# One tile of probabilities for the 64-row third chunks of a pair's two heads

## The chip, the cores and the metric

The kernel runs on 1 core of one Trainium2 chip. The metric is device time in microseconds (us) of one execution; 1089.18 is the median of three runs of the kernel before.

## The reference

Causal softmax attention over 4 x 8 heads of 576 positions with 64 columns each, mixed with a memory read-out by a gate per head, and behind it two feed-forward layers over 2304 tokens of 512 columns, with 2048 hidden units each:

```python
scores = scale * np.matmul(q, k.transpose(0, 1, 3, 2))      # then causal mask, minus the row's maximum
a = np.exp(scores)
a /= a.sum(-1, keepdims=True) + 1e-09
local = np.matmul(a, v)
q_p = phi(q)                                                # x > 0: x + 1, else exp(x)
mem_out = (q_p @ M_prev) / ((q_p * z_prev).sum(-1) + 1e-06)
attn = g * mem_out + (1 - g) * local                        # g = sigmoid(beta), one per head
h = x @ w_in;  x = elu(h) @ w_out                           # first layer
h = x @ w2_in; x = np.maximum(0.01 * h, h) @ w2_out         # second layer
```

## The kernel before

**Tiles.** The batch has four entries; in each, heads are taken in four pairs, 16 pairs in all. The 576 query rows of a head are cut into five chunks of 128, 128, 64, 128 and 128 rows (`CH`); the third has only 64. A pair's work falls into four *items*: for the first head chunks 0 and 1 (first group) and chunks 2, 3 and 4 (second group), and the same for the second head. So a pair's items are, in order, head 0 group 0, head 0 group 1, head 1 group 0, head 1 group 1.

**One item.** `score` makes for each chunk a matmul of queries and keys on PE (TensorE), a masked minimum on DVE (VectorE, line 431), which also writes the scores to the tile `pt`, and an exponential on ACT (ScalarE, line 436), which also sums each row. `norm` turns the sums into factors (rs, lines 445 and 446) and scales `pt` by them and by one minus the head's gate (`omg`) on POOL (GpSimd, line 451). `tr` transposes 128x128 pieces of `pt` on PE (line 457). In the second group `t1(0)`, `t1(1)` and `t1c` each transpose one block of keys of chunks 2, 3 and 4 into one bank, and the bank is split into a rounded part and a remainder by ACT and DVE (`ah`, `al`, `ac`, lines 247 to 250). `pv` multiplies them with the values (*value product*, line 524) and adds the memory read-out; its result goes to DRAM (`xq`). The first batch entry works in float32 without the split.

**Third chunk.** Its tile `pt2` holds 128 rows, of which 64 are used and the others stay zero. Each head has its own exponential, scaling and transposes for it.

**The first layer beside attention.** When a batch entry's attention is done, its tokens (two *parts* of 288 for each entry, parts 0 to 7) go through the first 7 blocks of hidden units of the first layer while the next entry's attention runs. A hidden unit is 12 matmuls on line 620, an output unit 21 on line 648. `u_load` brings the tokens in, `u_x` adds and rounds them (`xh`, `xl`, line 610). What is left over, and the rest of both layers with 512 tokens at a time, comes after attention. Weights are brought in as pairs of words and decoded by ACT, DVE and POOL (lines 112 to 137).

**Order.** The program lays units down one after another: `weave` mixes the scores of item n, the transposes of item n - 1 and the value product of item n - 2 by their place in their lists, and units of the first layer are put between them as the added costs of attention units give credit. From that a scheduler sets the order on each engine when the kernel is built, but an instruction marked to stay in program order (the first chunk's add and rounding in `u_x` and `split_x`) keeps its place. Each engine then works strictly in its order. DMAs are issued by SP (SyncE).

**Buffers.** `pt2` has two buffers, which alternate by item; `ah`, `al` and `ac` have two each, one for each item of the second group.

## Time and profile before

| | |
|---|---|
| median of 3 runs | 1089.18 us (1088.93 to 1090.98) |
| the profiled execution's own time | 1091.76 us |
| its span, first to last instruction | 1090.0 us |
| PE busy | 1052.7 us (97%) |
| DVE busy | 592.8 us (54%) |
| POOL busy | 527.5 us (48%) |
| ACT busy | 484.4 us (44%) |
| attention's last value product | at 394 us |
| mean granted clock of PE | 0.992 |

The clock of PE has two levels, 1.2 and 2.4 GHz; 1.00 is the higher one. PE counts as busy from a matmul's start to its modelled end, and ends overlap the next start, so what a matmul costs PE is read from the distance of starts. An idle time is followed by what ended it: "4.26 <-ACT xh L610" means that the engine had nothing to do for 4.26 us until ACT wrote xh on line 610.

### The profile page before, as it was taken

How to read it: one execution, taken by the hardware profiler on the slowest of the kernel's cores; microseconds unless marked ns; L12 is line 12 of the kernel's file. 1: busy time of each engine (PE TensorE's matmuls, PEld its weight loads, DVE VectorE, ACT ScalarE, POOL GpSimd, SP SyncE). 2: the span in 40 equal slices, each digit the busy share in tenths (PEclk: the TensorE clock that was granted, in tenths of full speed). 3: DMA queues.
4: the chain of work that ended last, by engine and by line, in shares of the span. 5: the costliest groups of instructions: out<-in, count | busy, mean ns of one | idle time of the engine just before them, and what ended most of it. 6: DMA issues, size and time to landing. Idle time of an engine off the chain costs nothing.

```text
span 1090.0 us, 17393 instructions
## 1 busy us (share of the span) xinstructions
PE 1052.7 (97%) x5904; PEld 912.6 (84%) x5904; DVE 592.8 (54%) x1398; ACT 484.4 (44%) x1169; POOL 527.5 (48%) x674
## 2 busy tenths in 40 slices
PE   6998999999999989999999999999999999999997
PEld 3786799989989989988777889888888888888896
DVE  6889987788878646566663214754321221232232
ACT  5899887777878534544342223432211211111110
POOL 7665776677667526555342234855422322222221
PEclk9999999999999999999999999999999999999999
DMA  7654543465445257666563304431200100000010
GB/s 181 186 150 113 161 141 98 123 167 147 119 122 145 88 168 228 219 207 203 170 208 97 112 5 117 142 112 37 78 1 1 58 20 1 6 34 1 1 39 20
DMA packets 151576, 115.05 MB, mean 106 GB/s; under 512 B 81728, under 2 KB 144192, under 8 KB 151488
## 3 DMA queue, kind: packets, MB, share of 16 engines
q1 hardware_dynamic: 151488, 113.95, 35.5%
q8 instruction: 47, 0.77, 0.3%
q14 instruction: 41, 0.34, 0.1%
HBM read 78.52 MB, written 31.85 MB: 101 GB/s over the span
## 4 chain that ended last, share of the span: by engine, by line
PE 74%; DVE 9%; DMA 8%; POOL 3%; issue 2%; ACT 2%; SPq 2%; DVEq 0%; POOLq 0%; ACTq 0%
PE pm L620 16%; PE sc L886 14%; PE tp L620 13%; PE sc L648 6%; PE pm L648 4%; PE po L886 4%; PE po L524 3%; PE tp L457 3%; DMA x1s<-st 2%; PE pm L524 2%; DMA y<-xq 2%; PE po L648 2%; PE sc L426 1%; PE sc L428 1%; DVE pt L431 1%
## 5 line engine op out<-in xcount | busy, mean ns | idle before, releaser
L627 POOL TENSOR_TENSOR gl<-e,gh 128x512 fp32r<-128x512 f32 (+2 forms) x181 | 198.2, 1097 | 383.8 <-DVE gh L243 287.0
L620 PE MATMUL tp<-xw,w 128*128 128x512 f32 (+1 forms) x504 | 145.1, 369 | 0.0
L620 PE MATMUL pm<-xw,w 128*128 128x512 f32 (+1 forms) x496 | 143.9, 371 | 0.4 <-DVE e L634 0.4
L886 PE MATMUL sc<-w,gh 128*128 128x512 f32 x448 | 137.6, 393 | 0.0
L451 POOL TENSOR_SCALAR pt<-pt,rs,omg 128x128 f32<-128x128 f32 (+4 forms) x160 | 101.9, 645 | 25.2 <-DVE rs L446 20.8
L648 PE MATMUL sc<-gh,w 128*128 128x512 f32 (+2 forms) x438 | 107.2, 343 | 3.3 <-DVE st L867 2.2
L620 PEld LDWEIGHTS pm<-xw,w 128*128 128x128 f32 x496 | 90.7, 188 | 18.2 <-DVE e L634 0.9
L620 PEld LDWEIGHTS tp<-xw,w 128*128 128x128 f32 x504 | 91.6, 188 | 16.8
L436 ACT ACTIVATE pt<-pt,mx 128x128 f32<-128x128 f32 (+4 forms) x160 | 93.1, 583 | 17.9 <-DVE mx L431 17.1
L886 PEld LDWEIGHTS sc<-w,gh 128*128 128x128 f32 x448 | 83.1, 188 | 17.8
L620 PE MATMUL tp<-xv,w 128*128 128x512 f32 (+1 forms) x252 | 92.7, 368 | 0.0
L620 PE MATMUL pm<-xv,w 128*128 128x512 f32 (+1 forms) x248 | 91.7, 370 | 0.0
L639 ACT ACTIVATE e<-pm 128x512 f32<-128x512 f32 (+1 forms) x40 | 22.2, 555 | 150.0 <-PE pm L620 148.6
L243 DVE CAST gh<-e 128x512 fp32r<-128x512 f32 (+2 forms) x146 | 76.7, 527 | 18.0 <-PE po L648 4.9
L648 PEld LDWEIGHTS sc<-gh,w 128*128 128x128 f32 x438 | 74.7, 188 | 13.9 <-issue 3.4
L886 PE MATMUL sc<-w,gl 128*128 128x512 f32 x224 | 85.4, 393 | 0.0
L457 PE MATMUL tp<-ident,pt 128*128 128x128 f32 x480 | 81.9, 281 | 3.4 <-ACT ah L247 2.1
L137 POOL TENSOR_TENSOR w<-wm,w 128x512 fp32r<-128x512 f32 x50 | 65.4, 1330 | 40.8 <-ACT w L241 40.2
L640 DVE TENSOR_TENSOR e<-tp,e 128x512 f32<-128x512 f32 (+1 forms) x40 | 25.5, 637 | 106.2 <-ACT e L639 106.0
L640 DVE TENSOR_TENSOR e<-pm,e 128x512 f32<-128x512 f32 (+1 forms) x40 | 25.5, 636 | 106.0 <-ACT e L639 106.0
L620 PE MATMUL pm<-xh,w 128*128 128x288 f32 x368 | 79.9, 305 | 0.3 <-DVE e L634 0.3
L431 DVE CUSTOM_DVE_ANT_0 pt<-sc,mask 128x128 f32<-128x128 f32 (+4 forms) x160 | 69.3, 446 | 8.6 <-PE sc L429 3.6
(155 smaller groups left out, 2400.3 us busy)
## 6 DMA issues: line engine op xcount, KB each, us to landing
wraw<-in_moe_w_in_dram SPq DMA_DIRECT2D x32, 512.0 KB, 4.1
wraw<-in_moe_w_out_dram SPq DMA_DIRECT2D x32, 512.0 KB, 5.2
xh<-xh SPq DMA_DIRECT2D x8, 576.0 KB, 3.1
xl<-xl SPq DMA_DIRECT2D x8, 576.0 KB, 3.8
ys<-st SPq DMA_DIRECT2D x32, 144.0 KB, 2.9
x1s<-st SPq DMA_DIRECT2D x36, 128.0 KB, 1.9
x<-x1s SPq DMA_DIRECT2D x9, 512.0 KB, 4.1
out_dram<-st SPq DMA_DIRECT2D x36, 128.0 KB, 1.7
```

The source lines that it names most:

```text
L137: nc.gpsimd.tensor_tensor(out=w[:, 1, a], in0=t[:, a], in1=_f(w)[:, 0, a], op=ALU.subtract)
L243: (nc.vector if eng == "V" else nc.gpsimd).tensor_copy(dst, src)
L431: nc.vector.tensor_tensor_reduce(out=pt[0:m, k0:k0 + n], in0=sc[0:m, 0:n], in1=mk, op0=ALU.add, op1=ALU.min, scale=-0.125, scalar=mx[0:m, ...
L436: nc.scalar.activation(out=pt[0:m, 0:nk], in_=pt[0:m, 0:nk], func=AF.Exp, scale=-1.0, bias=mx[0:m, last:last + 1], accum_out=self.pd["ss"] ...
L451: nc.gpsimd.tensor_scalar(out=pt, in0=pt, scalar1=rs[0:m, i:i + 1], scalar2=omg[0:m, h:h + 1], op0=ALU.mult, op1=ALU.mult,)
L457: nc.tensor.transpose(dst, self.p[c][:, k0:k0 + kn], ident)
L524: nc.tensor.matmul(po[:, a:b], w, x, start=i == 0, stop=i == len(mms) - 1)
L620: nc.tensor.matmul(ph, wi[:, wj, kc, :], xx[:, kc, :], start=n_mm == 0, stop=n_mm == 11)
L627: nc.gpsimd.tensor_tensor(out=gl, in0=g, in1=_f(gh), op=ALU.subtract)
L640: nc.vector.tensor_tensor(out=t, in0=ph, in1=t, op=ALU.max)
L648: nc.tensor.matmul(py, wo[:, wj, ec * P:(ec + 1) * P], gg, start=opens and f == first and n_mm == 0, stop=closes and f == last and n_mm == 2,)
L886: nc.tensor.matmul(pos[tb], gg[:, tb * P:(tb + 1) * P], wo[:, wj, :], start=f == 0 and n_mm == 0, stop=f == NF - 1 and n_mm == 2,)
```

## The change

The third chunks of both heads of a pair share `pt2`: head 0 in rows 0 to 63, head 1 in rows 64 to 127. Both score matmuls and minimums (`score2`) are done in the item of head 0 and group 1, and one exponential over 128 rows follows. One scaling over 128 rows takes a new table `omp`, which holds the gate factor of head 0 in the upper rows and that of head 1 in the lower. In `t1` and `t1c` the item of head 0 transposes the shared tile with chunks 3 and 4: the 64 columns of head 0 go to the front of the bank and those of head 1 to its end. The item of head 1 transposes only chunks 3 and 4. `ah`, `al` and `ac` belong to the pair: 640 columns, one buffer, written as 384 columns by head 0's item and as 256 by head 1's. The value products read 320 columns each, as before.

```diff
+    omp = const.tile([P, H // 2], F32, name="omp")
+    for j in range(2):
+        nc.vector.tensor_copy(omp[64 * j:64 * j + 64], omg.rearrange("p (h j) -> p j h", j=2)[64 * j:64 * j + 64, j])
...
+        def score2(self, j):
+            pr = self.pr
+            c0, m = CH[2]
+            nk = c0 + m
+            r = slice(64 * j, 64 * j + 64)
...
+            if j == 0:
+                self.p[2] = pads[self.n // 4 % 2]["pt2"]
+                self.mx2 = at.tile([P, 2], F32, tag="mx", bufs=4, name="mx")
+            pt, mx = self.p[2], self.mx2
+            sc = bank("sc")[:, 0:nk]
+            qc = qs[:, c0 - 64 * j:c0 - 64 * j + P]
...
+            o = 448 - c0 + 64 * j
+            nc.vector.tensor_tensor_reduce(
+                out=pt[r, 0:nk], in0=sc[r], in1=mask[r, o:o + nk], op0=ALU.add, op1=ALU.min,
+                scale=-0.125, scalar=1e38, accum_out=mx[r, 0:1],
+            )
+            if j == 1:
+                nc.scalar.activation(
+                    out=pt[:, 0:nk], in_=pt[:, 0:nk], func=AF.Exp, scale=-1.0, bias=mx[:, 0:1],
+                    accum_out=self.pd["ss"][:, 2:3],
+                )
...
+                og = omp[:, self.pr.hp:self.pr.hp + 1] if c == 2 else omg[:, h:h + 1]
                 nc.gpsimd.tensor_scalar(
-                    out=pt, in0=pt, scalar1=rs[0:m, i:i + 1], scalar2=omg[0:m, h:h + 1],
-                    op0=ALU.mult, op1=ALU.mult,
+                    out=pt, in0=pt, scalar1=rs[:, i:i + 1], scalar2=og, op0=ALU.mult, op1=ALU.mult,
                 )
...
+        def tr1(self, k0):
+            ps = bank("tp")
+            if self.j == 0:
+                self.tr(ps[:, 0:384].rearrange("p (b n) -> p b n", n=64)[:, 0:6:5], 2, k0, 128)
+            o = 64 if self.j == 0 else 0
+            for c in (3, 4):
+                self.tr(ps[:, o:o + P], c, k0, 128)
+                o += P
+            a = 384 * self.j
+            return ps[:, 0:o + 64 * (1 - self.j)], slice(a, a + o + 64 * (1 - self.j))
...
+            if kc == 0 and self.j == 0:
+                pr.ah = at.tile([P, 2, 640], F32R, tag="ah", name="ah")
+                pr.al = at.tile([P, 2, 640], F32R, tag="al", name="al")
+            split(pr.ah[:, kc, at_], pr.al[:, kc, at_], src, pr.full_v)
...
-            a = [(cost[c], lambda c=c: self.score(c)) for c in cc] + [(0, self.norm)]
+            a = [(cost[2], lambda j=j: self.score2(j)) for j in range(2)] if 2 in self.cc else []
+            a += [(cost[c], lambda c=c: self.score(c)) for c in cc if c != 2] + [(0, self.norm)]
```

The order on the engines changes with it. Three places follow.

POOL, the first pair, from the row factors of its second and third item on. Before:

```order
L445 TENSOR_SCALAR rs<-ss_152 128x3
L445 TENSOR_SCALAR rs<-ss_160 128x2
L243 COPY vv<-vn 128x640
L451 TENSOR_SCALAR pt_171<-pt_171,rs,omg 64x320
L451 TENSOR_SCALAR pt_309<-pt_309,rs,omg 128x448
L451 TENSOR_SCALAR pt_315<-pt_315,rs,omg 128x576
L396 TENSOR_TENSOR ph_e<-ph_f,den 128x640
```

The same place now:

```order
L474 TENSOR_SCALAR rs<-ss_155 128x3
L474 TENSOR_SCALAR rs<-ss_163 128x2
L399 TENSOR_TENSOR ph_e<-ph_f,den 128x640
L480 TENSOR_SCALAR pt_174<-pt_174,rs,omp 128x320
L480 TENSOR_SCALAR pt_315<-pt_315,rs,omg 128x448
L480 TENSOR_SCALAR pt_321<-pt_321,rs,omg 128x576
L246 COPY vv<-vn 128x640
```

The copy of the second pair's values (vv from vn, which a DMA brings) has moved behind the scaling of the second item.

PE, where the first hidden unit of part 2 begins (xh0_3628, on line 620, is its rounded tokens; dh0, dh1 and dh2 are the split tiles of three items in turn, here of the first, second and third item of the pair). Before:

```order
L457 MATMUL tp_3664<-ident_66,pt1_3482 128x128
L524 MATMUL po_3537<-qph_3467,ms1_183 128x256
L524 MATMUL po_3537<-qpl_3468,ms1_183 128x256
L524 MATMUL po_3537<-dh0_140,vv_3282 128x256
L524 MATMUL po_3537<-dh0_140,vv_3282 128x128
L524 MATMUL po_3537<-dl0_142,vv_3282 128x256
L524 MATMUL po_3537<-dl0_142,vv_3282 128x128
L428 MATMUL sc_3765<-kk0_3567,qs0_3655 128x256
L429 MATMUL sc_3765<-kl0_0_164,qs0_3655 128x256
L620 MATMUL pm_3670<-xh0_3628,w0_204 128x288 x2
```

The same place now, with the tokens xh0_3559 on line 658:

```order
L485 MATMUL tp_3819<-ident_66,pt1_3674 128x128
L561 MATMUL po_3681<-qph_3389,ms1_186 128x256
L561 MATMUL po_3681<-qpl_3390,ms1_186 128x256
L561 MATMUL po_3681<-dh2_159,vv_3206 128x256
L561 MATMUL po_3681<-dh2_159,vv_3206 128x128
L561 MATMUL po_3681<-dl2_161,vv_3206 128x256
L561 MATMUL po_3681<-dl2_161,vv_3206 128x128
L457 MATMUL sc_3855<-kk1_3484,qs1_3572 128x256
L458 MATMUL sc_3855<-kl1_0_169,qs1_3572 128x256
L658 MATMUL pm_3599<-xh0_3559,w0_207 128x288 x2
```

The hidden unit now comes after the value product of the pair's third item (dh2) and no longer after that of the first (dh0): the value products of two items have moved ahead of it.

ACT, right after attention: the rounding of part 6's tokens (xh_6577, three chunks together and then the first chunk, which keeps its place in the program), the decoding of a weight (wm, w) and copies of outputs of part 5 (st). Before:

```order
L610 CAST xh_6577<-x 128x288 x3
L126 ACTIVATE wm<-wraw 128x1024
L241 COPY st<-sc 128x288 x2
L610 CAST xh_6577<-x 128x288
L241 CAST w_6658<-wm 128x1024
```

The same place now:

```order
L648 CAST xh_6432<-x 128x288 x3
L129 ACTIVATE wm<-wraw 128x1024
L244 COPY st<-sc 128x288 x2
L244 CAST w_6513<-wm 128x1024
L244 COPY st<-sc 128x288 x2
L648 CAST xh_6432<-x 128x288
```

The first chunk's cast now stands behind all four output copies of part 5 and a weight's cast. Before, two of the four copies stood ahead of this whole place.

## Rows read from the trace of the kernel before

**Rows 1.** The page's totals: engine, busy us (share of the span), instructions.
```profile
PE 1052.7 (97%) x5904; PEld 912.6 (84%) x5904; DVE 592.8 (54%) x1398; ACT 484.4 (44%) x1169; POOL 527.5 (48%) x674
```
**Rows 2.** Busy us by window: length, PE, PEld, DVE, ACT, POOL, PEclk, DMA, GB/s.
```profile
100.00:110.00 10.00, 7.80 (x41) 5.70 (x40) 9.10 (x24) 9.19 (x26) 7.21 (x13) 0.83 0.63 157
...
120.00:130.00 10.00, 8.17 (x52) 7.13 (x52) 9.52 (x26) 8.07 (x23) 8.08 (x13) 0.83 0.57 159
```
**Rows 3.** Groups by line and shape: count | busy us, mean ns | idle before, releasers.
```profile
L457 PE MATMUL tp<-ident,pt 128*128 128x128 f32 x480 | 81.9, 281 | 3.4 <-ACT ah L247 2.1 <-DVE dl L250 0.4 <-DVE al L250 0.3
...
L436 ACT ACTIVATE pt<-pt,mx 128x448 f32<-128x448 f32 x32 | 21.4, 669 | 1.7 <-DVE mx L431 1.4
...
L436 ACT ACTIVATION_READ_ACCUMULATOR pt<-pt,mx 128x1 f32 x128 | 24.6, 193 | 0.0
...
L451 POOL TENSOR_SCALAR pt<-pt,rs,omg 64x320 f32<-64x320 f32 x32 | 19.5, 610 | 16.6 <-DVE rs L446 13.0 <-DVE den L394 1.2 <-DVE den L393 1.1
...
L436 ACT ACTIVATE pt<-pt,mx 64x320 f32<-64x320 f32 x32 | 17.9, 561 | 5.3 <-DVE mx L431 5.3
...
L436 ACT ACTIVATE pt<-pt,mx 128x256 f32<-128x256 f32 x32 | 16.3, 508 | 2.6 <-DVE mx L431 2.5
```
**Rows 4.** Timeline of PE, attention of the first entry: start us, duration us, instruction.
```profile
57.48 0.49 PE L457 MATMUL tp<-ident,pt 128*128 128x128 f32 x3
57.80 0.70 PE L524 MATMUL pm<-ah,vv 128*128 128x320 f32 x2
```
**Rows 5.** Timelines of ACT, PE and POOL at the start; in brackets idle time before.
```profile
24.34 0.65 ACT L112 ACTIVATE po<-wraw 128x512 f32<-128x512 f32 x1 [2.40 <-DMA wraw<-in_moe_w_in_dram]
...
28.19 1.11 PE L457 MATMUL tp<-ident,pt 128*128 128x128 f32 x4 [2.09 <-ACT ah L247]
...
21.25 0.72 POOL L243 COPY vv<-vn 128x640 f32<-128x640 f32 x1 [3.44 <-DMA vn<-in_v_dram]
21.95 2.10 POOL L451 TENSOR_SCALAR pt<-pt,rs,omg 64x320 f32<-64x320 f32 x3
```
**Rows 6.** Windows before parts 2 and 4; a chain piece of twelve 288-column matmuls.
```profile
216.40:228.60 12.20, 9.84 (x71) 8.22 (x70) 11.38 (x36) 10.92 (x32) 7.54 (x15) 1.00 0.44 117
320.70:327.70 7.00, 5.42 (x43) 4.71 (x41) 6.75 (x21) 5.90 (x17) 4.52 (x8) 1.00 0.52 141
...
391.13 1.60 PE pm L620 x12
```
**Rows 7.** End of attention: PE, ACT, the chain's store, store median (us), clock window.
```profile
393.91 0.40 PE L524 MATMUL po<-dl,vv 128*128 128x256 f32 x2
...
408.44 0.85 PE L620 MATMUL tp<-xh,w 128*128 128x288 f32 x2 [4.26 <-ACT xh L610]
...
405.20 1.12 ACT L126 ACTIVATE wm<-wraw 128x1024 f32<-128x1024 f32 x1 [1.43 <-DMA wraw<-in_moe_w_out_dram]
407.21 0.85 ACT L241 COPY st<-sc 128x288 f32<-128x288 f32 x2 [0.89 <-DMA ys<-st]
407.96 0.43 ACT L610 CAST xh<-x 128x288 fp32r<-128x288 f32 x1
...
399.62 7.48 DMA ys<-st
...
ys<-st SPq DMA_DIRECT2D x32, 144.0 KB, 2.9
...
408.00:412.00 4.00, 3.56 (x15) 3.56 (x16) 1.53 (x2) 1.44 (x3) 2.98 (x2) 0.50 1.07 337
```
**Rows 8.** Timeline of DVE near the start: start us, duration us, instruction.
```profile
8.46 0.08 DVE L431 DVE_READ_ACCUMULATOR2_ANT mx<- 128x1 f32 x1
8.57 0.49 DVE L243 COPY q<-sc 64x320 f32<-64x320 f32 x1
...
12.12 0.08 DVE L431 DVE_READ_ACCUMULATOR2_ANT mx<- 64x1 f32 x1
12.12 0.68 DVE L114 SCALAR_TENSOR_TENSOR po<-wraw,po 128x512 int32<-128x512 int32 x1
```

More of the change, by code (lines that the diff above doesn't have):

```diff
@@ L408, in __init__ @@
             self.n = n
+            self.cc = [c for c in grp[3] if c != 2 or j == 0]
             self.p = {}
+        def score2(self, j):
[3 more added lines that the diff above has]
+            r = slice(64 * j, 64 * j + 64)
+            qs, kk, kl = pr.qs[j], pr.kk[0 if pr.full_v else j], pr.pad["kl", j]
+            if j == 0:
[4 more added lines that the diff above has]
+            qc = qs[:, c0 - 64 * j:c0 - 64 * j + P]
+            if pr.full_v:
+                nc.tensor.matmul(sc, qc, _f(kk)[:, 0:nk], start=True, stop=True)
+            else:
+                nc.tensor.matmul(sc, qc, kk[:, 0:nk], start=True, stop=False)
+                nc.tensor.matmul(sc, qc, kl[:, 0:nk], start=False, stop=True)
+            o = 448 - c0 + 64 * j
[8 more added lines that the diff above has]
+                )
         def score(self, c):
@@ L416, in score @@
             spans = [(0, nk, nk)] if c < 4 else [(0, 288, 288), (288, 288, 288)]
-            if c == 2:
-                pt = self.p[c] = pads[self.n // 2 % 2]["pt2"]
-            else:
-                pt = self.p[c] = at.tile([P, nk], F32, tag=f"pt{c}", bufs=2, name=f"pt{c}")
+            pt = self.p[c] = at.tile([P, nk], F32, tag=f"pt{c}", bufs=2, name=f"pt{c}")
             mx = at.tile([P, 2], F32, tag="mx", bufs=4, name="mx")
@@ L471, in t0 @@
             self.split_d(ps)
-        def t1(self, kc):
-            ps = bank("tp")
-            for c in (2, 3, 4):
-                o = CH[c][0] - 256
-                self.tr(ps[:, o:o + P], c, 128 * kc, 128)
-            if kc == 0:
-                self.ah = at.tile([P, 2, 320], F32R, tag="ah", bufs=2, name="ah")
-                self.al = at.tile([P, 2, 320], F32R, tag="al", bufs=2, name="al")
-            split(self.ah[:, kc, :], self.al[:, kc, :], ps[:, 0:320], self.pr.full_v)
+        def tr1(self, k0):
[8 more added lines that the diff above has]
+            return ps[:, 0:o + 64 * (1 - self.j)], slice(a, a + o + 64 * (1 - self.j))
+        def t1(self, kc):
+            pr = self.pr
+            src, at_ = self.tr1(128 * kc)
+            if kc == 0 and self.j == 0:
+                pr.ah = at.tile([P, 2, 640], F32R, tag="ah", name="ah")
+                pr.al = at.tile([P, 2, 640], F32R, tag="al", name="al")
+            split(pr.ah[:, kc, at_], pr.al[:, kc, at_], src, pr.full_v)
         def t1b(self):
@@ L490, in t1c @@
         def t1c(self):
-            ps = bank("tp")
-            for c in (2, 3, 4):
-                o = CH[c][0] - 256
-                self.tr(ps[:, o:o + P], c, 256, 128)
-            ct = self.ac = at.tile([P, 320], F32R, tag="ac", bufs=2, name="ac")
-            if self.pr.full_v:
-                nc.gpsimd.memset(_f(ct)[64:128], 0.0)
-            split(ct[0:64], ct[64:128], ps[0:64, 0:320], self.pr.full_v)
+            pr = self.pr
+            src, at_ = self.tr1(256)
+            if self.j == 0:
+                pr.ac = at.tile([P, 640], F32R, tag="ac", name="ac")
+                if pr.full_v:
+                    nc.gpsimd.memset(_f(pr.ac)[64:128], 0.0)
+            split(pr.ac[0:64, at_], pr.ac[64:128, at_], src[0:64], pr.full_v)
         def pv(self):
@@ L513, in pv @@
             else:
-                for a in (self.ah,) if full else (self.ah, self.al):
+                js = slice(320 * j, 320 * j + 320)
+                for a in (pr.ah,) if full else (pr.ah, pr.al):
                     for kc in range(2):
-                        mms.append((0, n, pr.vc[j, kc], a[:, kc, :]))
-                mms.append((0, n, pr.vc[j, 2], self.ac))
+                        mms.append((0, n, pr.vc[j, kc], a[:, kc, js]))
+                mms.append((0, n, pr.vc[j, 2], pr.ac[:, js]))
                 for a in ("d32",) if full else ("dh", "dl"):
```

7 lines of the change are left out of this document (3 added, 4 removed).

## The prediction

> **What bounds the kernel now.** I began with the engine totals: PE is busy for 1052.7 of 1090.0 us, nearly twice as long as DVE, the next [rows 1]. So whatever comes off PE should come off the time, unless PE is waiting where it comes off. The totals can't tell that, and I read the first 420 us, where attention runs, in slices [rows 2]. Most slices have PE full. In three places it is not: the start, the stretch around 86 to 127 us, and the short stretches in which the fill of the first MLP has run dry and PE has attention alone. There DVE is the engine that is nearly always busy (9.10 and 9.52 of 10 us), so PE's own work doesn't set the pace. Two stretches of that kind come later, just before the first hidden unit of part 2 and of part 4; there DVE is busy for 11.38 of 12.20 and 6.75 of 7.00 us [rows 6]. Last I read the end of attention, where PE is idle for 4.26 us [rows 7].
>
> **The change part by part.** Durations are those of the one profiled execution; its span is 1090.0 us and its time 1091.76, and the median of the runs is 1089.18, so I work out a difference and take it from the median.
>
> *Transposes.* A head's second group had 3 chunks x 3 transposes over the third chunks and the rest (and 3 of another kind, which stay). Now the first head has 9 and the second 6: 3 fewer for each of 16 pairs, 48 of the 480 [rows 3]. Such a row lasts 281 ns, but they are pipelined. Three of them hold PE from 57.48 to 57.80 [rows 4], 0.107 us each. 48 x 0.107 = **5.1 us less** on PE. The score matmuls keep number and size, and the splits of 320 + 320 columns become 384 + 256, the same columns.
>
> The new transposes write two blocks of 64 columns that lie apart. No row shows such a write. If it costs as much as before, nothing changes; if each block cost as much as a transpose, 48 x 0.107 = 5.1 us would come back. I take zero, as the number of columns is the same 128.
>
> *ACT and POOL.* 32 exponentials of 64x320 become 16 of 128x320. One takes 561 ns plus 193 ns for reading its sum. Rows don't matter and columns do: from 128x256 (508) to 64x320 (561) to 128x448 (669) it grows by 0.83 and 0.84 ns a column [rows 3]. So ACT loses 16 x 0.75 = 12 us of work, and POOL 16 x 0.61 = 9.8 us. Almost all of it lies beside PE work, where it is worth nothing. Only in the stretches that DVE paces could it help, and there four pairs at most pass: between 0 and 4 x 0.75 = 3.0 us. I take zero, because DVE is the fuller engine there. The new exponential waits for the second head's minimum, but PE and ACT have other work queued there.
>
> *DVE.* The two small copies for the new table stand where DVE waits for ACT's first copy of a query; without that cover they would cost two of DVE's shortest operations, 0.2 us once. The minimum of the second head's chunk now works on partitions 64 to 127. The trace shows what that does: the copy into partitions 64 to 127 at 8.57 starts 0.03 us after the instruction ahead of it has ended, while the usual successor at 12.12 starts 0.08 before that end [rows 8]. So 0.11 is lost on the way there and as much on the way back, 0.2 us a pair, 3.2 us of DVE in all. Where PE is full this is hidden. I count it for three pairs that pass through the paced stretches, **+0.6 us**, between 0 and 3.2.
>
> The Trainium skill has a rule for this (VectorE: DVE Perf Modes, section "Two Vector instructions with no wait between them"): an instruction whose operands start in another quadrant of 32 partitions than the last one's starts only when all earlier Vector instructions have finished. The trace agrees, with its 0.11 us at 8.57 [rows 8]. Read by that rule alone, with all 16 pairs paying in the time, the sum below would be 2.6 us higher, -1.6 + 2.6 = +1.0; PE's full slices speak against that.
>
> *The stretch to the first hidden unit.* While DVE paces (86 to 127 us), transposes that go bring nothing. About two pairs pass: 6 x 0.107 = **+0.6 us** given back, between 0 and 1.1.
>
> *The start.* POOL waits 3.44 us for a DMA of values, and the scaling of the second group, which PE waits for, stands behind it [rows 5]. In the new order that scaling stands ahead of the copy (first order fences). So up to 3.4 us could go, but then PE comes to its wait for ACT (2.09 us at 28.19 [rows 5]), and ACT still waits for the weights that land at 24.34 [rows 5]. I take **-1.0 us**, half of what PE waits there, between 0 and -2.1.
>
> *Two stretches with attention alone.* In the new order the first hidden unit of part 2 stands behind the value product of the third item of its pair, not of the first (second fences); before part 4 likewise. I counted each instruction of these stretches at its own pace (a transpose 0.107; a matmul of 288 columns 0.133, from 12 in 1.60 us [rows 6], others by their columns). Before, they hold 7.8 and 4.4 us of PE work and took 12.20 and 7.00, so 7.0 us were lost on 12.2, 0.57 for each us of work. Now they hold 12.5 and 7.1, 7.4 us more, taken out of stretches in which it lay beside MLP work. 7.4 x 0.57 = **+4.2 us**. The bounds are 0, and 7.6 where the clock falls too: at 100 to 110 and 120 to 130 the granted clock averages 0.83 [rows 2], which takes 1.7 us of ten, and twice that is 3.4.
>
> *The end of attention.* The last value product ends at 394.31 and the next hidden unit starts at 408.44 [rows 7], 14.1 later. Of those, PE had 9.9 of output matmuls. The unit waits for the cast of its first chunk, which stands on ACT behind two output copies, and these behind a store of 7.48 us [rows 7]. In the new order PE has 14.7 us of work there, as the last items come earlier. But on ACT four copies and a weight cast stand ahead of that cast (third fences), and two of the copies need outputs that are now ready only some 12 us after the last value product. The weight activation ends at 406.32, 12.0 after the last value product. Two copies (0.85) follow, then a store of 2.9 us (the median of such stores) to 7.48, two copies (0.85) and the cast (0.43) [rows 7]: the unit starts 17.0 to 21.6 us after it, and PE is idle for 2.3 to 6.9 us. I take 3.4, nearer the lower end, since the weight loads that delayed the store are further on by then: 3.4 for 4.3 is **-0.9 us**, between -2.0 and +2.6. The slow clock after it (0.50 [rows 7]) stays. Behind this point PE has the same work as before.
>
> The shared split tiles have one buffer a pair in place of two: the next pair's first split waits for the last value product of the pair before, which stands ahead of its transposes on PE anyway. That costs nothing; if it were not so, PE would wait in the mixed slices, which are full now.
>
> Sum: -5.1 + 0.6 + 0.6 - 1.0 + 4.2 - 0.9 = **-1.6 us**, so 1087.6 us.
>
> **The rivals.** *Faster:* the two stretches cost nothing extra, because ACT with its 12 us less, and not DVE, was what they waited for (ACT is at 10.92 and 5.90 in them [rows 6]). Then the 4.2 falls away and the time is 1083.4. For it speaks that work is taken from the bounding engine. Against it speaks that the waits in these stretches name DVE (its minimum, its qs) and that DVE is the fuller one.
>
> *Slower:* the store at the end of attention again takes its 7.48 us, so that PE idles for 6.9 us (+3.5 over my value), and in one of the two longer stretches the clock falls as it does at 100 to 130 us (+1.7). That gives 1092.8, and 1094.5 with both. It decides once the two add up to 3.8 us, with one fall of the clock from a store of some 6 us. Against it speaks that the clock stayed at 1.00 in both stretches before [rows 6].
>
> *It doesn't do what it says:* the split writes cost as two transposes. Then 5.1 comes back and the time is 1092.7. Nothing in the trace speaks for it.
>
> **How the numbers follow.** A difference under 0.2%, 2.2 us, is about what a measurement of this kernel can't tell from none. My forecast of 1087.6 lies within it, with its own range of 1087.0 to 1091.4, and has 0.44. The faster rival, from about half of the 4.2 falling away downwards, has 0.37; slower 0.16 by the end of attention and the clock and 0.03 by the split writes. The range goes from 1082.5 (the faster rival with the rest of the start's wait gone) to 1093.0 (the slower one): some 1 in 10 lies below and as much above.
>
> **What would show it.** The transpose line must show 432 in place of 480, and the split ones no longer spaced than 0.107 us. The idle time of PE between the last output matmul of part 1 and the first hidden unit of part 2 should grow, with DVE full and its waits naming DVE; if it doesn't grow, the faster rival is right. POOL's scaling of the first pair's second group should start before 21 us. The idle time before the first hidden unit of part 6 should be 2 to 6 us, and the wait should name ACT's cast. I am wrong in kind if PE's slices between 130 and 350 us are no longer full outside those stretches.

## The result and the profile after

The changed kernel takes 1102.26 us (median of 4 runs, 1101.17 to 1103.05) against 1089.06 for the kernel before beside it. The ratio is 1.0119 with a 95% interval of 1.0098 to 1.0140: slower by some 13 us, where 1087.6 with a range of 1082.5 to 1093.0 was predicted. The profiled executions took 1101.74 and 1091.76 us, so the traces show 10 of the 13 us; the profiled one of before was 2.7 us slower than its median.

First the terms that came out as planned. The page's totals and the groups by line and shape of the kernel after, which answer to [rows 1] and [rows 3]:

```profile
PE 1056.6 (96%) x5856; PEld 908.8 (83%) x5856; DVE 595.3 (54%) x1400; ACT 478.8 (44%) x1137; POOL 519.5 (47%) x654
...
L485 PE MATMUL tp<-ident,pt 128*128 128x128 f32 x432 | 78.5, 280 | 5.5 <-DVE al L253 2.3 <-ACT ah L250 1.3 <-POOL pt L480 0.6
...
L480 POOL TENSOR_SCALAR pt<-pt,rs,omp 128x320 f32<-128x320 f32 x16 | 9.8, 612 | 3.1 <-DVE rs L475 2.0 <-ACT pt L465 0.3 <-POOL ms L246 0.2
...
L438 ACT ACTIVATE pt<-pt,mx 128x320 f32<-128x320 f32 x16 | 9.0, 564 | 5.4 <-DVE mx L433 5.2
```

There are 432 transposes of 280 ns, 16 joint exponentials of 564 ns and 16 joint scalings of 612 ns, within 3 ns of what one of 64 rows took [rows 3]. Yet PE is busy for longer (1056.6 against 1052.7) and idle for longer (43.1 against 37.3).

Where the time went is read from the starts of each part's first hidden unit on PE's timeline. Beside them stands PE's work ahead of that point, counted as in the prediction at each instruction's own pace; start minus work is what PE has lost up to there, by waiting or by a slower clock. (How much work is ahead depends on the pace taken for each shape; the last column hardly does.)

| first hidden unit of | start before | after | PE work ahead, before | after | lost, before | after | more lost by now |
|---|---|---|---|---|---|---|---|
| (second value product) | 31.5 | 28.3 | 13.6 | 13.5 | 17.9 | 14.8 | -3.1 |
| part 0 | 127.0 | 130.4 | 93.2 | 92.1 | 33.8 | 38.3 | +4.5 |
| part 1 | 171.7 | 173.1 | 137.0 | 133.6 | 34.7 | 39.5 | +4.9 |
| part 2 | 228.6 | 239.7 | 187.5 | 189.8 | 41.1 | 49.9 | +8.8 |
| part 3 | 273.2 | 283.1 | 230.7 | 229.2 | 42.5 | 53.9 | +11.4 |
| part 4 | 327.7 | 340.0 | 280.0 | 279.4 | 47.7 | 60.6 | +12.9 |
| part 6 | 408.4 | 415.8 | 352.8 | 347.6 | 55.7 | 68.3 | +12.6 |
| part 7 | 428.8 | 438.7 | 370.7 | 365.9 | 58.1 | 72.8 | +14.7 |

At the end 14.9 us more are lost and 5.2 us of PE work are gone: 9.7, the difference of the spans. So the transposes did pay their 5 us, and the rest is lost. The clock is no part of it in sum: over the first 465 us, added up from windows of 5 us, the lower clock took 8.5 us in either kernel. Half of the loss, 7.6 us from the second value product on, arises before part 0. Counted in the same way at a value product at 86 us, the changed kernel is still 0.5 us ahead: 2.6 us are lost up to there, and 5.0 in the stretch behind it, which the prediction priced at +0.6.

In that stretch a wait stands that the kernel before does not have. ACT's timeline of the kernel after around 100 us, then DVE's, PE's weight loads' and PE's:

```profile
100.16 0.37 ACT L252 CAST qph<-po 128x256 fp32r<-128x256 f32 x1 [0.27 <-PE po L333]
102.78 0.43 ACT L648 CAST xh<-x 128x288 fp32r<-128x288 f32 x1 [2.25 <-DMA x<-xm]
103.24 0.81 ACT L303 CAST kk<-sc 64x256 fp32r<-64x256 f32 x2
103.95 0.76 ACT L648 CAST xh<-x 128x288 fp32r<-128x288 f32 x2
104.62 0.78 ACT L465 ACTIVATE pt<-pt,mx 128x576 f32<-128x576 f32 x1
```

```profile
103.64 0.94 DVE L305 TENSOR_TENSOR kl<-sc,kk 64x256 fp32r<-64x256 f32 x2 [2.41 <-ACT kk L303]
...
104.12 0.51 PEld L342 LDWEIGHTS sc<-ident,qn 128*128 128x128 f32 x3 [1.48 <-DVE kl L305]
...
104.12 0.90 PE L342 MATMUL sc<-ident,qn 128*128 128x128 f32 x3 [1.08 <-DMA vn<-in_v_dram]
...
106.77 0.58 PE L561 MATMUL po<-qph,ms 128*128 128x256 f32 x1 [1.32 <-DVE qpl L253]
```

The first part's input (`x`) is rounded by four casts, one for each chunk. Only the first chunk's is kept in program order (`if c == 0: tc.keep_in_program_order(hi)`); the other three may be put anywhere, it seems where the scheduler takes the load for landed. Here one of them stands in front of attention's key casts (`kk`), which are needed at once, and two more right behind these. The load lands after ACT has waited for 2.25 us. DVE waits for the key cast, and PE behind both: its row at 104.12 names a DMA, but the weight load of the same matmuls names DVE's `kl`, which waited for ACT. In ACT's timeline of the kernel before, the same three casts have no wait:

```profile
108.49 1.10 ACT L610 CAST xh<-x 128x288 fp32r<-128x288 f32 x3
```

There 17 instructions (the reads of the accumulator not counted) stand in ACT's queue between the last copy that the load depends on and these casts, now 8.

The Trainium skill says of ACT, DVE and POOL that their queues are "strict FIFO" (PSUM — Partial Sum Buffer, section "Engine vs sequencer instructions"). The trace agrees: `kk` starts only at 103.24, behind the cast that waited.

Like waits stand on DVE, where the two halves of a part's input are added (line 719). Parts 3 and 5, on DVE's timeline of the kernel after, and PE's wait behind the first:

```profile
247.98 0.08 DVE L460 DVE_READ_ACCUMULATOR2_ANT mx<- 128x1 f32 x1
250.00 1.99 DVE L719 TENSOR_TENSOR x<-x,y 128x288 f32<-128x288 f32 x3 [1.94 <-issue]
251.91 0.44 DVE L672 SCALAR_TENSOR_TENSOR e<-e,pm 128x288 f32<-128x288 f32 x1
...
351.46 1.20 DVE L719 TENSOR_TENSOR x<-x,y 128x288 f32<-128x288 f32 x3 [2.73 <-DMA y<-xq]
```

```profile
252.41 0.53 PE L658 MATMUL pm<-xh,w 128*128 128x288 f32 x2 [1.79 <-DVE e L672]
```

The first row names no releaser; by the view of the loaded tensor (`xq`) it was the load. In sum these waits are as long as before: 1.9, 1.9, 0.9 and 2.7 us for parts 2 to 5, against 2.0, 1.3, 1.6 and 2.4. What differs is what stood behind them: PE waits 2.6 us for DVE's `e` at 240 to 262 us, and before 0.3 us at 238 to 250. Whether these places are the cause, the experiments had to show.

### The profile page after: what moved, and what is told of

Its sections match the earlier page's. It is cut to its first block, busy times and chain, and to the rows that moved or that the text cites. A ratio compares the mean times of both kernels' runs of the same rounds, so it can differ in the third digit from the quotient of the medians.

```text
span 1099.7 us, 17255 instructions
## 1 busy us (share of the span) xinstructions
PE 1056.6 (96%) x5856; PEld 908.8 (83%) x5856; DVE 595.3 (54%) x1400; ACT 478.8 (44%) x1137; POOL 519.5 (47%) x654
## 4 chain that ended last, share of the span: by engine, by line
PE 78%; DVE 6%; DMA 6%; ACT 4%; issue 3%; SPq 2%; POOL 1%; DVEq 0%; ACTq 0%; POOLq 0%
PE pm L658 18%; PE tp L658 15%; PE sc L924 14%; PE sc L686 9%; PE po L924 4%; PE pm L686 4%; PE po L561 3%; PE tp L485 3%; PE po L686 3%; DMA x<-xq 2%; PE pm L561 1%; DMA wraw<-in_moe_w_out_dram 1%; SPq L217 1%; PE sc L457 1%; PE sc L458 1%
## 5 line engine op out<-in xcount | busy, mean ns | idle before, releaser
L665 POOL TENSOR_TENSOR gl<-e,gh 128x512 fp32r<-128x512 f32 (+2 forms) x181 | 199.0, 1102 | 391.3 <-DVE gh L246 325.9
L480 POOL TENSOR_SCALAR pt<-pt,rs,omg 128x128 f32<-128x128 f32 (+3 forms) x128 | 83.5, 663 | 22.1 <-DVE rs L475 21.3
L465 ACT ACTIVATE pt<-pt,mx 128x128 f32<-128x128 f32 (+3 forms) x128 | 75.3, 589 | 29.1 <-DVE mx L460 26.3
L140 POOL TENSOR_TENSOR w<-wm,w 128x512 fp32r<-128x512 f32 x50 | 65.7, 1334 | 38.7 <-ACT w L244 33.8
L485 PE MATMUL tp<-ident,pt 128*128 128x128 f32 x432 | 78.5, 280 | 5.5 <-DVE al L253 2.3
L677 ACT ACTIVATE e<-tp 128x512 f32<-128x512 f32 (+1 forms) x40 | 22.2, 555 | 119.1 <-PE tp L658 116.6
```

The lines of the kernel that those rows point to most:

```text
L140: nc.gpsimd.tensor_tensor(out=w[:, 1, a], in0=t[:, a], in1=_f(w)[:, 0, a], op=ALU.subtract)
L465: nc.scalar.activation(out=pt[0:m, 0:nk], in_=pt[0:m, 0:nk], func=AF.Exp, scale=-1.0, bias=mx[0:m, last:last + 1], accum_out=self.pd["ss"] ...
L480: nc.gpsimd.tensor_scalar(out=pt, in0=pt, scalar1=rs[:, i:i + 1], scalar2=og, op0=ALU.mult, op1=ALU.mult,)
L485: nc.tensor.transpose(dst, self.p[c][:, k0:k0 + kn], ident)
L665: nc.gpsimd.tensor_tensor(out=gl, in0=g, in1=_f(gh), op=ALU.subtract)
L677: nc.scalar.mul(t, ph, 0.01)
```

## The experiments

All ratios are to the kernel before, run beside each on the same chip.

**Early casts.** The tie: all four casts of a part's input, and all four additions, are kept in program order. It was made in the changed kernel, in the kernel before, and in the changed kernel for the first part's casts alone.

```diff
-            if c == 0:
-                tc.keep_in_program_order(hi)
+            tc.keep_in_program_order(hi)
...
-                    if c == 0:
-                        tc.keep_in_program_order(add)
+                    tc.keep_in_program_order(add)
```

> The changed kernel; all four casts of a part's input (and all four additions of its halves) are tied behind one another in program order, where only the first was, so that chunks 2 to 4 can no longer stand earlier in ACT's and DVE's queues than the scheduler's guess of the load allows. Theory 'early casts': in the changed kernel ACT waits 2.25 us at 100.5 us for the load of part 0, DVE 1.94 us at 248 us for that of part 3 and 2.73 us at 348.7 us for that of part 5, with attention's work queued behind, and PE stands still. Without these waits about 5 to 9 us come back: 1093 to 1097 us against 1102.3. Theory 'attention alone' (all of the loss is in the stretches that DVE paces before parts 2 and 4 and before part 0): no change, 1101 to 1103 us.

> The kernel before with the same tie of all four casts and additions, as control. Theory 'early casts': before, the same waits stand at 200.8, 240.5, 303.3 and 340.1 us (2.0, 1.3, 1.6 and 2.4 us) but hardly anything on PE hangs on them, so the tie gives little: 1086 to 1090 us against 1089. Theory 'attention alone': the same, 1088 to 1090.

> The changed kernel; the four casts are tied behind one another for the first part only, and everything else stays as in the changed kernel. Theory 'early casts': ACT's 2.25 us wait at 100.5 us and the fall of the clock behind it (granted clock 0.72 and 0.76 at 96 to 106 and 106 to 116) go, part 0's first hidden unit starts 5 to 6 us earlier (130.4 before), and about that much of the 9.0 us of the full tie comes back: 1095.5 to 1098 us. Rival: the 9.0 us came from the later parts: 1101 to 1103.

Tied, the changed kernel takes 1093.24 us (1.0039, 1.0026 to 1.0052): 9.0 of the 13 us are back, as the theory had it. With the first part alone it takes 1099.16 (1.0087, 1.0074 to 1.0100), 3.1 back, less than expected. The place itself behaves as expected: part 0 starts at 124.5 and not at 130.4. But behind it the order is another one again: between parts 2 and 3 it loses 4.5 us more than the kernel before, where the changed kernel lost 2.6 more. Its profiled execution is 2.0 us faster than its median, so its trace shows more of the gain than the runs do. Windows of the changed kernel, then of the one with all casts tied: length, PE, PEld, DVE, ACT, POOL busy, granted clock, DMA, GB/s.

```profile
96.00:106.00 10.00, 6.71 (x29) 4.32 (x27) 6.37 (x24) 7.41 (x23) 7.57 (x12) 0.72 0.52 126
106.00:116.00 10.00, 8.59 (x44) 7.24 (x44) 9.09 (x24) 7.38 (x19) 4.62 (x8) 0.76 0.39 94
```

```profile
96.00:106.00 10.00, 7.28 (x47) 5.56 (x47) 9.26 (x31) 9.53 (x27) 7.07 (x14) 1.00 0.64 156
106.00:116.00 10.00, 8.50 (x56) 6.94 (x55) 9.60 (x34) 6.98 (x21) 4.54 (x8) 1.00 0.37 100
```

In the same 20 us PE does 103 matmuls instead of 73, and the clock stays at its higher level; with the wait it stood at the lower level for half of the time. But the wait did not start that. Shorter windows of the changed kernel, then of the one with the first part's casts tied (columns as above):

```profile
95.00:100.00 5.00, 3.59 (x20) 2.26 (x19) 5.00 (x19) 4.82 (x14) 2.14 (x4) 1.00 0.11 21
100.00:105.00 5.00, 3.67 (x18) 2.98 (x17) 2.14 (x9) 2.55 (x7) 4.43 (x7) 0.55 0.84 210
```

```profile
100.00:105.00 5.00, 3.52 (x23) 2.95 (x24) 4.19 (x11) 4.90 (x12) 4.03 (x7) 0.92 0.82 215
105.00:110.00 5.00, 5.00 (x29) 4.76 (x29) 4.78 (x15) 3.02 (x10) 2.33 (x4) 0.74 0.51 125
```

A clock of 0.55 means that the lower level began at 100.5, when ACT had just begun to wait and PE did not yet wait for it; ahead of it PE was busy for 3.59 of 5 us. With the first casts tied there is such a stretch too, of some 3 us in place of 10. So the wait can have made the slow stretch longer; that it did is argued, as the order ahead of it differs a little as well.

The control was the surprise: tied, the kernel *before* takes 1099.14 us (1.0096, 1.0071 to 1.0121), 10 us more, where 1086 to 1090 was expected. As long as attention runs it hardly waits for loads any more, but the clock falls in three stretches (columns as above):

```profile
120.00:130.00 10.00, 8.26 (x40) 7.83 (x40) 8.54 (x19) 7.40 (x20) 6.70 (x12) 0.66 0.35 89
222.00:232.00 10.00, 7.60 (x37) 6.06 (x36) 9.78 (x27) 8.25 (x22) 4.75 (x9) 0.71 0.50 125
332.00:340.00 8.00, 7.38 (x34) 7.26 (x35) 4.93 (x15) 5.11 (x13) 3.42 (x6) 0.58 0.92 282
```

They cost 3.4, 2.9 and 3.4 us (length times one minus the clock), of which before had 1.7 in the first stretch alone. So the tie is no remedy, and the 9.0 us that it gave back cannot all be put down to the waits that it takes away. It makes another order, good for one kernel and bad for the other. And with the tie in both kernels the change makes the kernel *faster*: 1093.24 against 1099.14, a ratio of 0.994 with some 0.003 either way.

**One order or the change?** That called for more pairs: both kernels with the same number of the planner altered, so that both get another order. DELAY says how much planned attention work passes before units of the first layer are handed out.

```diff
-    DELAY = 13000.0
+    DELAY = 11000.0        # and, in a second pair, 15000.0
```

> The kernel before with one number of the planner altered (DELAY 13000 to 11000: MLP units are handed out some 2 us of planned work earlier after a sequence half is done); its instructions are those of before. Half of a pair: the question is what the change does when both kernels get another order. No theory names its time closely: 1088 to 1102.

> The changed kernel with the same number altered (DELAY 11000). Theory 'one order's luck': the change's own terms (5.1 us of transposes off PE, 0.24 us of DVE for each pair on) give a difference to the kernel before with the same number of -6 to +3 us, as with the casts tied (1093.2 against 1099.1); the 13 us belong to the one order of DELAY 13000. Rival 'the change itself': it is 8 to 18 us slower than its partner here too.

> The kernel before with DELAY 15000, partner of the next. 1089 to 1106.

> The changed kernel with DELAY 15000. Theory 'one order's luck': -6 to +3 us against its partner. Rival 'the change itself': 8 to 18 us slower than its partner.

The last pair has three numbers altered:

```diff
-    SHIFT = {"prep": 0.0, "score": -0.3, "tr": 0.0, "pv": -0.1}
+    SHIFT = {"prep": 0.0, "score": -0.4, "tr": 0.2, "pv": -0.1}
...
-    PC = 200
+    PC = 100
...
-    RESERVE = 60000.0
+    RESERVE = 50000.0
```

> The kernel before with the same altered numbers of the planner (casts as before), as control. If the altered plan suits the kernel before as well, 1080 to 1086 us; theory 'order' (the numbers fit one order of work and not another): 1090 to 1102.

> The changed kernel with the altered numbers of the planner (RESERVE 50000, PC 100, SHIFT of the scores -0.4 and of the transposes +0.2), casts free and the cost as the change books it: partner of the kernel before with the same numbers, 1106.3 us. Theory 'one order's luck': -6 to +3 us against the partner, 1100 to 1109. Rival 'the change itself': 1114 to 1124.

| order | kernel before | changed kernel | difference, by the two ratios |
|---|---|---|---|
| as it is | 1089.06 | 1102.26 | +13.0 (10.7 to 15.2) |
| casts tied | 1099.14 | 1093.24 | -6.2 (-9.3 to -3.1) |
| DELAY 11000 | 1095.31 | 1095.90 | +0.2 (-3.1 to 3.5) |
| DELAY 15000 | 1100.77 | 1103.85 | +2.6 (-0.6 to 5.8) |
| three numbers altered | 1106.28 | 1107.25 | +0.5 (-2.8 to 3.8) |

The interval of a pair is worked out from the two ratios' intervals, added as independent. The rival that the change itself costs 8 to 18 us falls: in four orders of five the difference lies between -6.2 and +2.6 us, with a mean of -0.7. Three of the four intervals reach to 3.5, 3.8 and 5.8 us, so a cost of a few us is not excluded. What stands out is the kernel before in its own order: 1089 where its other four orders take 1095 to 1106. The changed kernel's 1102 lies in the middle of its five.

**DVE's hold at the upper partitions.** The kernel before, with the second head's third chunk in partitions 64 to 127; every engine's order stays as it was.

```diff
+            u = 64 * j if c == 2 else 0
+            q0, r = c0 - u, slice(u, u + m)
...
-                    out=pt[0:m, k0:k0 + n], in0=sc[0:m, 0:n], in1=mk, op0=ALU.add, op1=ALU.min,
+                    out=pt[r, k0:k0 + n], in0=sc[r, 0:n], in1=mask[r, mo:mo + n], op0=ALU.add, op1=ALU.min,
```

> The kernel before with one part of the change alone: the second head's third chunk is worked on in partitions 64 to 127 (minimum, exponential, scaling), with its own transposes; the instructions and their order on every engine stay as they were. Prediction's step on DVE: about 0.2 us of DVE for each of 16 pairs, +0.6 us in time (0 to 3.2): 1089 to 1090. Rival 'the hold of DVE is what the change loses': +3 us or more, 1092 or above. Theory 'early casts': no loss here, 1088 to 1090.

It takes 1092.71 us (1.0029, 1.0017 to 1.0041): 3.2 us, not 0.6. DVE's timeline of this kernel, a minimum of the first head (161.50) and one of the second (171.90), each with its neighbours:

```profile
161.11 0.47 DVE L250 TENSOR_TENSOR al<-tp,ah 128x320 fp32r<-128x320 f32 x1
161.50 0.47 DVE L433 CUSTOM_DVE_ANT_0 pt<-sc,mask 64x320 f32<-64x320 f32 x1
161.91 0.07 DVE L433 DVE_READ_ACCUMULATOR2_ANT mx<- 64x1 f32 x1
161.91 0.38 DVE L393 SCALAR_TENSOR_TENSOR den<-den,ging 128x10 f32<-128x10 f32 x1
...
171.40 0.47 DVE L250 TENSOR_TENSOR al<-tp,ah 128x320 fp32r<-128x320 f32 x1
171.90 0.50 DVE L433 CUSTOM_DVE_ANT_0 pt<-sc,mask 64x320 f32<-64x320 f32 x1
172.33 0.08 DVE L433 DVE_READ_ACCUMULATOR2_ANT mx<- 64x1 f32 x1
172.44 0.49 DVE L250 TENSOR_TENSOR al<-tp,ah 128x320 fp32r<-128x320 f32 x1
```

The second head's minimum starts 0.03 us after its predecessor's end instead of 0.08 before it, takes 0.02 longer, and its successor comes 0.11 us after the accumulator read instead of with it: 0.24 us. Nine of the 16 pairs lose that much; in the others DVE had started late at one of these places before as well, and added up over the 16 pairs it is 3.0 us. The rule of the Trainium skill that the prediction weighed (VectorE: DVE Perf Modes, section "Two Vector instructions with no wait between them") held in all 16 pairs, and an amount like the whole came into the time (3.2, between 1.9 and 4.5). In the trace 1.0 us of it is lost by part 0, and 1.5 between parts 1 and 3. There the clock falls once more than before; windows of this kernel, then of the kernel before in the same stretch (columns as above):

```profile
222.00:232.00 10.00, 7.65 (x45) 6.11 (x44) 9.57 (x29) 8.86 (x25) 6.18 (x10) 0.88 0.54 149
232.00:242.00 10.00, 10.00 (x76) 9.96 (x75) 7.36 (x25) 6.40 (x18) 6.38 (x10) 0.95 0.92 252
```

```profile
220.00:230.00 10.00, 7.64 (x54) 6.10 (x54) 9.48 (x29) 8.55 (x24) 6.38 (x11) 1.00 0.53 141
230.00:240.00 10.00, 10.00 (x80) 9.96 (x80) 8.53 (x29) 7.78 (x25) 7.56 (x13) 1.00 0.93 257
```

0.12 and 0.05 of ten us are the 1.7 us that the prediction had put on one fall of the clock, but only in a bound and in its slower rival. How much of the 3.2 us is the hold itself and how much this fall, the one trace does not tell.

**The planner's bookkeeping.** In the changed kernel, the cost of the second head's third chunk is booked in that head's item again, as before; nothing else. Then the same with the casts tied.

```diff
+            own = (220, 220, 280, 390 + 280 * self.j, 490)
-            a = [(cost[2], lambda j=j: self.score2(j)) for j in range(2)] if 2 in self.cc else []
-            a += [(cost[c], lambda c=c: self.score(c)) for c in cc if c != 2] + [(0, self.norm)]
+            a = [(cost[2] * (1 - j), lambda j=j: self.score2(j)) for j in range(2)] if 2 in self.cc else []
+            a += [(own[c], lambda c=c: self.score(c)) for c in cc if c != 2] + [(0, self.norm)]
```

> The changed kernel; only the planner's bookkeeping is altered: the 280 ns of the second head's third chunk are booked on the second head's next score, where they were before, so that the fill of MLP units keeps its old pace. The first hidden unit of part 2 then stands behind value product 36 and not 39, and that of part 4 behind 53 and not 55 (before: 37 and 52). Theory 'attention alone': these two stretches lose some 4 to 5 us less, 1097 to 1098.5 us. Theory 'early casts': the casts of part 0 keep their place, so at most the waits at 248 and 349 us move: 1098 to 1103.

> The changed kernel with both: the cost of the second head's third chunk booked where it was, and all four casts and additions of a part tied together. If the two gains (9.0 and 7.0 us of the 13.2) are of different places, 1087 to 1090 us; if they take the same waits away, 1092 to 1094.

The first takes 1095.26 us (1.0053, 1.0035 to 1.0071), 7.0 less than the change, by a number that no engine sees. From the last output matmul of part 1 to part 2's first hidden unit it needs 11.3 us instead of 20.1, as the theory said; the stretch before part 4 grew from 11.5 to 17.0. The time came out below what either theory expected. With the tie it takes 1092.97 (1.0027, 1.0018 to 1.0037), no better than the tie alone: the two gains do not add.

**Parts of the change.** The kernel before with both heads' third chunks scored in the first head's item, and nothing shared; and the changed kernel with separate transposes.

```diff
-            a = [(cost[c], lambda c=c: self.score(c)) for c in cc] + [(0, self.norm)]
+            a = [(cost[c], lambda c=c: self.score(c)) for c in cc if c != 2] + [(0, self.norm)]
+            if 2 in cc and self.j == 0:
+                a = [(cost[2], lambda it=it: it.score(2)) for it in (self, self.mate)] + a
...
```

> The kernel before with one part of the change alone: both heads' third chunks are scored in the first head's item (their cost is booked there too); each keeps its own tile, its own exponential, scaling and transposes in the low partitions. PE's work is that of before. Theory 'order': most of the loss comes from the new places of the work in the queues, so this alone loses 6 to 12 us: 1095 to 1101 us. Rival 'sharing': the loss comes from the joint exponential, the pair's tiles and the upper partitions, and this stays within 2 us of before, 1087 to 1091.

```diff
         def tr1(self, k0):
...
             if self.j == 0:
-                self.tr(ps[:, 0:384].rearrange("p (b n) -> p b n", n=64)[:, 0:6:5], 2, k0, 128)
...
+                self.pr.pt2 = self.p[2]
+            self.p[2] = self.pr.pt2
...
+            self.tr(ps[:, 0:P], 2, k0, 128)
...
-                pr.ah = at.tile([P, 2, 640], F32R, tag="ah", name="ah")
...
+                self.ah = at.tile([P, 2, 320], F32R, tag="ah", bufs=2, name="ah")
...
```

> The changed kernel with one part undone: each head transposes the shared tile of probabilities for itself (480 transposes again, split tiles of 320 columns with two buffers as before); scores, exponential and scaling stay shared. If the 48 transposes are worth 5.1 us and nothing else moves: 1107 us. If what the transposes save is lost in waits anyway (theory 'attention alone'): 1102 to 1104. If the pair's single-buffered split tiles cost something: below 1102. Theory 'order': here the first part's early casts stand behind 11.5 us of other work on ACT and not 4.7, so some 4 us come back from there: 1100 to 1104.

The order alone takes 1124.70 us (1.0317, 1.0298 to 1.0337), far outside what either theory expected. It is not a clean test: the second head's tile is written two items earlier, and DVE now waits for the transposes of the pair before to let go of it. The waits of DVE in this kernel (us in total, times, longest):

```profile
DVE pt L431 <- PE tp L457: 7.4, 8, 2.2
```

The changed kernel's shared tile has two buffers over pairs, and this wait is not among its large ones. The 7.4 us are a small part of the 35; what the rest is was not followed, so this run settles nothing. The kernel with separate transposes takes 1112.40 (1.0203, 1.0189 to 1.0218), 10.1 more than the change and more than any theory expected, where 5.1 was the price on PE. The sign is that of the prediction. In its trace the lower clock took 13.7 us of the first 465, 5.2 more than in the change, which is the size of the other 5 us; what lowered it was not followed. That it is slower without the strided writes and the single-buffered pair tiles speaks against both as a cost, but weakly, as its order is another one too. More direct is the distance of starts from one transpose to the next: 0.109 us (median) in the changed kernel, also from the first to the second of three, where the strided ones stand, and 0.109 in the kernel before. The single buffer has no test of its own.

**One minimum for both heads.** Both heads' scores go into one bank, and one minimum of 128 rows takes the place of two of 64 (the mask is laid out anew for it, the shared tile is 320 columns wide, and its last transpose has 64). It was run with the casts tied; with the casts tied, the three planner numbers and the bookkeeping above; and with free casts, half of the cost booked so and a further set of numbers. The partner of the second has its numbers and ties, but two minima.

```diff
+            for j in (1, 0):
+                qc = pr.qs[j][:, c0 - 64 * j:c0 + m]
...
+                o = sc[0:64 + 64 * j]
...
             nc.vector.tensor_tensor_reduce(
...
+                out=pt[:, 0:nk], in0=sc, in1=mask[:, 0:nk], op0=ALU.add, op1=ALU.min,
...
```

> The changed kernel with the four casts tied, and one minimum for both heads' third chunks: both heads' scores are written into one PSUM bank (the second head's first, the first head's 64 rows over it), and one DVE instruction of 128 rows takes the place of two of 64. DVE loses 16 instructions of some 0.49 us and the hold at partitions 64 to 127, 11 us of its work in all. Theory 'hold': at least the 3.2 us that the upper partitions cost alone come back against 1093.2: 1088 to 1090. Theory 'DVE paces' (attention alone at DVE's pace): another 2 to 4 us: 1085 to 1088. If DVE is not what matters: 1092 to 1094.

> The changed kernel with one minimum for both heads, the four casts tied, the second head's cost booked where it was, and the planner's numbers altered so that hidden units are handed out earlier and transposes later in an item (RESERVE 60000 to 50000, PC 200 to 100, SHIFT of the scores -0.3 to -0.4 and of the transposes 0 to +0.2). Theory 'order': where the work stands decides some 10 us in either direction, so with this other plan DVE's 11 us less can come through: 1080 to 1087 us. Rival 'DVE's work is not what the stretches wait for': like the kernel with one minimum and the old plan, 1100 to 1106.

> The changed kernel with the casts tied, the cost booked where it was, and the same altered numbers of the planner as in the run with one minimum, but with the two minima of the change. If the plan alone makes the gain: 1082 to 1088. If it needs DVE's 11 us less too: 1091 to 1098.

> The changed kernel with one minimum for both heads (DVE 11 us less, no hold at partitions 64 to 127), casts free, half of the second head's cost booked in its own item, and a third set of planner numbers (RESERVE 55000, PC 100, SHIFT prep +0.05, scores -0.4, transposes +0.2, value products 0). If an order suits it as the old one suits the kernel before, 1080 to 1087 us; if orders differ by some 4 us about the mean of those seen with one minimum (1091 and 1105), 1088 to 1102.

The minimum itself does what it should; its group in the first of these kernels:

```profile
L436 DVE CUSTOM_DVE_ANT_0 pt<-sc,mask 128x320 f32<-128x320 f32 x16 | 7.8, 484 | 3.2 <-PE sc L435 2.1 <-PE sc L432 0.9
```

Sixteen of 484 ns in place of 32 of 486. But the times are 1105.13 (1.0135, 1.0119 to 1.0152) with the old numbers, 1090.91 (1.0014, 1.0000 to 1.0028) with the new ones against 1097.76 (1.0085, 1.0073 to 1.0098) for two minima, and 1105.03 (1.0148, 1.0125 to 1.0170) with the further ones. The first and the last lie above what was expected for them, and the second above what the theory of the order gave it. With the same numbers the one minimum gains 6.9 us; against the tied change with the old numbers it loses 10.5 by the two ratios. In the last kernel the clock was at its lower level for 15 us on end, which alone is 7.5 us:

```profile
100.00:115.00 15.00, 12.17 (x49) 9.93 (x49) 11.43 (x34) 10.97 (x31) 6.79 (x12) 0.50 0.35 88
```

No version ran faster than the kernel before; the best one comes to it within the measurement.

## Why the prediction was wrong

*The stretch to the first hidden unit, +0.6.* This step failed, and it is the largest. The prediction counted there only the transposes that bring nothing, 0 to 1.1 us, and took all other work for as well placed as before. 5.0 us more were lost there. The wait for the first part's early cast stands in it, with the lower clock over 96 to 116 us; with the first part's casts tied, part 0 starts 5.9 us earlier.

*Transposes, -5.1.* Right: 432, the writes of two blocks cost nothing extra, and PE's own work is 5.2 us less.

*ACT and POOL, zero.* Right in the instructions taken away (16 x 0.75 and 16 x 0.61 us; busy time as the page counts it fell by only 5.6 us on ACT and 8.0 on POOL), and no gain shows. What the prediction did not see is that a less loaded ACT also has its holes elsewhere, into which the scheduler puts the early casts; that this is why they moved is argued, not shown.

*DVE's hold, +0.6.* Mis-sized. It is 0.24 us and not 0.2 for a pair, and the step "I count it for three pairs" failed: 3.2 us came into the time, the upper bound, 1.7 of them probably by one fall of the clock in part 2's stretch. The rule of the Trainium skill read alone, which the prediction set aside because PE's slices are full, was nearer.

*The start, -1.0.* The order of POOL changed as said, but the time was not as said: its scaling starts at 23.19 us, not before 21, since POOL waited for DVE's factor until 21.94. Still, PE's wait of 2.09 us for ACT [rows 5] is gone, and 3.1 us are won by the second value product, more than the bound of 2.1. By part 0 it had all been lost again, and 4.5 us more.

*Two stretches with attention alone, +4.2.* Right in kind and size. Windows of the kernel after from the last output matmul of parts 1 and 3 to the next hidden unit, which answer to [rows 6]:

```profile
219.60:239.70 20.10, 16.54 (x113) 13.37 (x112) 19.21 (x60) 15.14 (x43) 12.37 (x24) 1.00 0.41 108
328.50:340.00 11.50, 9.29 (x67) 7.61 (x65) 10.35 (x27) 9.67 (x26) 5.90 (x10) 1.00 0.46 108
```

DVE is busy for 19.21 of 20.10 and 10.35 of 11.50 us and the clock stays up; the table has 3.9 and 1.5 us more lost between parts 1 and 2 and parts 3 and 4, 5.4 in all. So the faster rival is refuted here.

*The end of attention, -0.9.* Nearly right: PE is idle for 2.3 us, the wait names ACT's cast, and it stands behind two copies and a store, as the answer to [rows 7] shows; but 2.1 us are lost again before part 7.

```profile
415.84 0.53 PE L658 MATMUL tp<-xh,w 128*128 128x288 f32 x2 [2.32 <-ACT xh L648]
```

```profile
413.20 1.04 ACT L244 CAST w<-wm 128x1024 fp32r<-128x1024 f32 x1 [2.48 <-DVE wm L134]
414.67 0.79 ACT L244 COPY st<-sc 128x288 f32<-128x288 f32 x2 [0.43 <-DMA ys<-st]
415.36 0.43 ACT L648 CAST xh<-x 128x288 fp32r<-128x288 f32 x1
```

*What was not in the sum.* Behind the failed step stands a silent one: that outside the places I priced, and for all but the transposes within them, the new order loses what the old one lost. The prediction's test of kind was whether PE's slices between 130 and 350 us stay full outside the two stretches. They do not quite: at 248 us PE waits behind part 3's additions, and 2.6 us more are lost between parts 2 and 3. As much was lost between the start and 86 us, where nothing was priced either. I had the rows to ask for it: casts that may be put anywhere, the load in front of them, and the second order fence, which showed that units move by whole items.

The slower rival had the wrong mechanism (a store at the end, which took no part). The pairs say how the forecast would have had to look. The terms of the change itself, priced from the trace, gave -1.6 us, and four other orders give -0.7 in the mean. Around that the orders scatter: the changed kernel's five reach from 1093 to 1107 us, some 7 us either way, and the kernel before stands at the good end of its scatter, 6 to 17 us ahead of its other orders. Whether that is chance, or its numbers were chosen for it, no run tells. A range of 1082.5 to 1093.0 could not hold that.

What stays open: what makes the one order of the kernel before so good; why it loses 10 us by the tie, which was read as three falls of the clock but not followed to what PE waited for; and the 4.3 us that the tied change still lacks are not divided between hold, stretches and order.

## What to carry to other kernels

When an edit feeds a planner or a scheduler, price the new order as a cost of its own: run both versions in a few orders (one planner number altered in both) before crediting or blaming the edit, since one pair alone had here +13 us and another -6. Look in the new order for every instruction that waits for a load and was allowed to move, and for what stands behind it in its engine's queue. An operation in other partitions is not free on DVE even where the engine is half idle over the whole kernel: count it for all its instances as the upper bound, and take that bound seriously where other stretches run at DVE's pace.

## What the hardware showed unexpectedly

Around a wait of 2.25 us on ACT a part started 5.9 us later than with its casts tied, and PE's clock was at 0.72 and 0.76 over 20 us, against 1.00 with all casts tied. Over the first 465 us the time lost to the lower clock was 8.5 us in the kernel before, 8.5 in the changed one and 15.3 in the tied kernel before: of the ten us that this one lost, 6.8 are clock. An instruction of DVE in partitions 64 to 127 between two in the lower ones costs 0.24 us where DVE would have run on. And a transpose that writes two blocks of 64 columns costs what one block of 128 does, 0.109 us.
